# TensorE's loop over head pairs written out as straight code, with deeper buffers for weights and probabilities

## The chip, the cores and the metric

The kernel runs on one core of a Trainium2 chip. The metric is the device time of one execution in microseconds, as the median of several runs. One execution was also taken by the hardware profiler; its time and its span are given beside the median.

## What is computed

One decode step of an attention layer and an MLP in parallel, for 8 sequences with one token each. The model width D is 640, there are 32 heads of 128, 32 key and value heads, a cache of 4096 positions, and an MLP of 1728.

```
xn  = layernorm(x)
q   = (xn @ wq) as 8 x 32 heads x 128
s   = q . k_cache * 128**-0.5          # 8 x 32 x 4096
p   = softmax(s)
o   = p . v_cache                       # 8 x 32 x 128
y   = layernorm(xn)
h   = gelu(y @ w1 + b1)
out = x + o @ wo + h @ w2 + b2
```

All inputs and the output are bfloat16. Each key and value is used once, by one query, so nearly all of the 552 MB that are read are the two caches, 268 MB each.

## The kernel before

**Tiles.** A tile t (0 to 127) is one sequence and one pair of heads (HT = 2): 2 MB of K and 2 MB of V, on 128 partitions, 64 positions of 128 on each, in rows of 16 KB. The eight sequences of one head pair are eight tiles that follow each other; there are 16 head pairs (NG). Four tiles make a group (GT), whose softmax is done together; two groups make a head pair.

**Buffers.** KV_sb holds four K tiles and four V tiles (NK, NV). The V part is lent at first to the weights of the queries and of the MLP. wo_sb holds the rows of wo of one head pair. P_sb holds the probabilities of PR = 2 groups, S_sb the scores of three.

**Scores of a tile** (`scores`). VectorE makes the scores of 48 of the 64 positions: it multiplies the K tile with the query spread over the partitions (L534, into Y_sb), adds the halves (L538) and reduces (L541). TensorE makes those of the other 16: it transposes eight K blocks at a time (L502, into TR_ps), ScalarE copies them out (L505), and TensorE multiplies with the query (L512). The query for VectorE is broadcast by TensorE (`qbcast`, L471) from qb_sb; that for TensorE is read from qk_sb. Both are copies of the head pair's part of qT_sb, made on ScalarE by `qcopy` (L484).

**Softmax of a group** (`softmax`). VectorE takes the maximum (L549), TensorE transposes it (L551), VectorE reduces (L553), TensorE spreads it (L558), and ScalarE does the exponentials (L568). TensorE sums the parts (L579) and VectorE takes the reciprocal (L584, rinv_sb).

**Values of a tile** (`values`). Sixteen matmuls of 512 columns (L605), in four steps q of four, go into PV_ps; ScalarE copies it to E_sb (L613), and TensorE gathers the blocks into the output of the group (L621). The last tile of all loads its V in four pieces and uses 64 narrow matmuls of 128 columns (L602) with one gather (L619).

**Finish** (`finish`). VectorE scales the group's output (L629, oTn_sb). After each head pair but the last TensorE projects it through wo into an accumulator, transposed (L647). Before the last head pair is done, the accumulator with all other heads and the MLP is copied (L695), transposed back (L700), added to x and b2 (L707) and put into rows again (L713). The last head pair is projected straight onto those rows (L637), and the rows go out (L717, L719, L721).

**Order.** The order on each engine is fixed when the program is built. Each step has a position on one line of tile numbers: K tile t is loaded at t - 3.6 and scored at t; the values of tile i stand at `pvpos(i)`, which is 6.2 + i; V tile i + 4 is loaded at `pvpos(i)` + 0.95; wo of head pair hg is loaded at 8 hg + 7.2. `_Sched.solve` sorts the steps by position and works out the waits between engines. SP's queue issues all loads of K, V and the large weights in that order, each when its buffer is free: a K load waits for the scores of the tile four before, a V load for the values of the tile four before.

**TensorE's loop.** All engines run their steps as straight code, but TensorE doesn't. `emit_rolled` cuts TensorE's steps into windows of one head pair (eight positions, from 6.43), finds the longest run of windows that are alike, and writes that window once as the body of a loop. The values that its waits need rise by the same amount from window to window, so they are held in registers:

```
with e.Fori(0, j - i + 1):
    for o in body:
        for key, val in self.needs(o).items():
            e.reg_add(regs[key], regs[key], val - at[key])
            at[key] = val
            e.wait_ge(sems[key], regs[key])
        self.issue(o, e, sems)
```

The loop runs 15 times and takes in most of the scores and values; what stands ahead of it (the weights' work and the first tiles) and behind it (the last tiles) is straight code.

Of the kernel before, what the change touches and what calls it, by code (L numbers as in the profile page):

```python
# [6 lines left out]
BF = mybir.dt.bfloat16  # L7
# [4 lines left out]
P = 128  # L12
# [7 lines left out]
class _Sched:  # L20
# [79 lines left out]

    @staticmethod
    def needs(o):
        best = {}
        for d in o.waits:
            key = d.eng if d.sem is None else ("dma", d.sem)
            best[key] = max(best.get(key, 0), d.ticket)
        return best

    def emit(self, eng, e, sems, only=None):
        for o in self.ops if only is None else only:  # L110
            if o.eng != eng:
                continue
            for key, val in self.needs(o).items():
                e.wait_ge(sems[key], val)
            self.issue(o, e, sems)

    @staticmethod
    def issue(o, e, sems):
        last = o.fn(e)
        if o.sig:  # L120
            if o.sem is not None:
                last.then_inc(sems[("dma", o.sem)], 16)
            else:
                last.then_inc(sems[o.eng], 1)

    def emit_rolled(self, eng, e, sems, p0, step):

        ops = [o for o in self.ops if o.eng == eng]
        wins = {}
        for o in ops:
            if o.pos >= p0 and o.pos < 1e8:
                wins.setdefault(int((o.pos - p0) // step), []).append(o)

        def shape(w):
            return [(o.fn.__code__.co_firstlineno, o.sig, tuple(self.needs(o))) for o in w]  # L140

        def rise(a, b):
            return [tuple(nb[k] - na[k] for k in na) for na, nb in zip(map(self.needs, a), map(self.needs, b))]

        best = (0, 0)
        n = max(wins) + 1 if wins else 0
        for i in range(n):
            j = i
            while j + 1 < n and shape(wins[j + 1]) == shape(wins[i]) and (
                    j == i or rise(wins[j], wins[j + 1]) == rise(wins[i], wins[i + 1])):  # L150
                j += 1
            if j - i > best[1] - best[0]:
                best = (i, j)
        i, j = best
        if j - i < 2:
            self.emit(eng, e, sems)
            return
        body = wins[i]
        first, last = ops.index(body[0]), ops.index(wins[j][-1])
        self.emit(eng, e, sems, ops[:first])  # L160
        up = {}
        for o, r in zip(body, rise(body, wins[i + 1])):
            for key, d in zip(self.needs(o), r):
                assert up.setdefault(key, d) == d
        at = {}
        for o in body:
            at.update(self.needs(o))
        regs = {}
        for key in up:
            regs[key] = e.alloc_register("w%d" % len(regs))  # L170
            at[key] -= up[key]
            e.reg_mov(regs[key], at[key])
        with e.Fori(0, j - i + 1):
            for o in body:
                for key, val in self.needs(o).items():
                    e.reg_add(regs[key], regs[key], val - at[key])
                    at[key] = val
                    e.wait_ge(sems[key], regs[key])
                self.issue(o, e, sems)
        self.emit(eng, e, sems, ops[last + 1:])  # L180

# [19 lines left out]
def bass_parallel_sum__gqa_block_cached__mixer_channel_mlp__decode_kernel(  # L201
# [32 lines left out]
    NK, NV, NS = 4, 4, 4  # L234
    PR, SR = 2, 3
    assert DH == P and D % P == 0 and H % HT == 0 and B == 8 and NJ == 64 and H % 4 == 0
# [4 lines left out]
    with ExitStack() as es:  # L241
# [5 lines left out]
        KT_sb = sb("KT_sb", [P, NS, BK, P], BF)  # L247
        wo_sb = sb("wo_sb", [P, HT, D], BF)
        b1_sb = sb("b1_sb", [1, F], BF)
# [7 lines left out]
        qT_sb = sb("qT_sb", [P, H, B], BF)  # L257
        qb_sb = sb("qb_sb", [P, HT, B], BF)
        qk_sb = sb("qk_sb", [P, HT, B], BF)
        qbc_sb = sb("qbc_sb", [P, 2, GT, P], BF)  # L260
# [21 lines left out]
        rinv_sb = sb("rinv_sb", [P, 2, HT * GT], F32)  # L282
        oTn_sb = sb("oTn_sb", [P, HT, B], BF)
        resT_sb = sb("resT_sb", [P, DC * B], F32)
# [75 lines left out]
        def ld(pos, dst, src, W, sem, R=()):  # L360
            add("sp", pos, lambda e: e.dma_start(dst, src), R=R, W=W, sem=sem)
# [5 lines left out]
        if H > QP:  # L367
            ld(1.9, wqb_sb, A_wq[:, QP * P:H * P].rearrange("(c k) n -> k c n", k=P), ["wqB"], "wqb", ["ovfree"])

        def pvpos(i):  # L370
            return 6.2 + i

# [19 lines left out]
        for hg in range(NG):  # L392
            ld(hg * B + 7.2, wo_sb[:, :, :],
               A_wo[hg * HT * P:(hg + 1) * HT * P, :].rearrange("(a p) n -> p a n", p=P), ["wo"],
               "wo")

# [66 lines left out]
        def qbcast(g):  # L463
            hg, b0 = g // GPH, (g % GPH) * GT
            pos = g * GT - 1.3 if g else -55.0
            it = TRR.item()

            def pe(e):
                for i in range(GT):
                    for a in range(HT):  # L470
                        r = e.matmul(TRF[a * PG:(a + 1) * PG, it.box[0], i * P:(i + 1) * P],  # L471
                                     qb_sb[:, a, b0 + i:b0 + i + 1].to_broadcast([P, PG]),
                                     ident_bf[:, :], start=True, stop=True)
                return r
            add("pe", pos, pe, R=["qb", "ident"], W=[it], X=[it])
            add("act", pos + .01, lambda e: e.activation(  # L476
                qbc_sb[:, g % 2, :, :].rearrange("p g d -> p (g d)"), TRF[:, it.box[0], :], ACT.Copy),
                R=[it], W=[("qbc", g % 2)], X=[it])
        for g in range(NGRP):
            qbcast(g)  # L480


        def qcopy(hg, pos, dst, res):
            add("act", pos, lambda e: e.activation(dst[:, :, :], qT_sb[:, hg * HT:(hg + 1) * HT, :], ACT.Copy),  # L484
                R=[qt_res(hg * HT)], W=[res])
        for hg in range(NG):
            qcopy(hg, hg * B - 1.62 if hg else -56.0, qb_sb, "qb")
            qcopy(hg, hg * B - 0.62, qk_sb, "qk")


        def scores(t):
# [4 lines left out]
            def bank(n):  # L496
# [12 lines left out]
                def pe_qk(e):  # L509
                    for jj in range(BK):  # L510
                        c = (n * BK + jj) * HT
                        r = e.matmul(S_ps[:, c:c + HT], KT_sb[:, m % NS, jj, :],  # L512
                                     qk_sb[:, :, b], start=True, stop=True)
                    return r
                add("pe", t - 0.25 + 0.2 * n, pe_qk, R=[("KT", m % NS), "qk"], W=["S"], X=["S"])
            for n in range(MP):
# [109 lines left out]
        def finish(g):  # L626
            hg, b0 = g // GPH, (g % GPH) * GT
            np_ = pvpos(g * GT + GT - 1) + 0.85
            add("dve", np_, lambda e: e.tensor_tensor(  # L629
                oTn_sb[:, :, b0:b0 + GT], OT_ps.rearrange("p (a g) -> p a g", a=HT),  # L630
                rinv_sb[:, g % 2, :].rearrange("p (a g) -> p a g", a=HT), ALU.mult),
                R=["OT", ("rinv", g % 2)], W=["oTn"], X=["C2"])
            if g == NGRP - 1:
                def pe_last(e):
                    for a in range(HT):
                        for k in range(2):
                            r = e.matmul(TRF[0:B, k, 0:D // 2], oTn_sb[:, a, :],  # L637
                                         wo_sb[:, a, k * D // 2:(k + 1) * D // 2], start=False,
                                         stop=(a == HT - 1), skip_group_check=True)
                    return r  # L640
                add("pe", np_ + 0.3, pe_last, R=["wo", "oTn", "base_ps"], W=["fin"],
                    X=[("TR", 0), ("TR", 1)])
            elif (g + 1) % GPH == 0:
                def pe_o(e):
                    for a in range(HT):
                        for c in range(DC):
                            r = e.matmul(ACC_ps[:, c * B:(c + 1) * B], wo_sb[:, a, c * P:(c + 1) * P],  # L647
                                         oTn_sb[:, a, :], start=False,
                                         stop=(hg == NG - 2 and a == HT - 1 and c == DC - 1), skip_group_check=True)
                    return r  # L650
                add("pe", np_ + 0.32, pe_o, R=["wo", "oTn"], W=["ACC"], X=["ACC"])
        for t in range(T):
# [80 lines left out]
        @block.tensor  # L733
        def _(e):
            sch.emit_rolled("pe", e, sems, 6.43, B)

# [35 lines left out]
```

## Time and profile before

| | us |
|---|---|
| median of 3 runs | 1309.41 (1309.4 to 1309.8) |
| profiled execution, its own time | 1309.8 |
| its span, first to last instruction | 1308.0 |
| VectorE busy | 1111.0 (85%) |
| TensorE matmuls busy | 702.6 (54%) |
| ScalarE busy | 516.7 (39%) |
| read from HBM | 551.80 MB, 422 GB/s over the span |

A line of the page's DMA part has a queue, its kind, its packets, its megabytes, and the time that its packets took as a share of the span of all 16 DMA engines. A line of waits has the engine and line that waited, what it waited for, the total in microseconds, how often, and the longest. A piece of the chain has its start and its length in microseconds, the engine, the tile that it wrote, and the line.

### The profile page before, as it was taken

Reading aid. Unit: us, or ns where it says so; the run is one execution under the profiler, and the core shown is the slowest. Engines: PE = TensorE matmul, PEld = TensorE weight load, DVE = VectorE, ACT = ScalarE, POOL = GpSimd, SP = SyncE. Lnnn points to the kernel's source line nnn. Section 1 sums busy time; section 2 is a strip of 40 time slices with the busy share of each in tenths; the row PEclk is TensorE's granted clock in tenths of the full one; section 3 lists DMA queues with packets and bytes.
Section 4 is the critical chain, followed back from the end, with each engine's and each line's share of the span. In section 5 each row is a group of like instructions: output and inputs, shape, how many; then the busy total and the mean of one; then the engine's idle time right before and its main releaser. Section 6 shows DMA issues by size and latency. Waiting matters only on the chain.

```text
span 1308.0 us, 18464 instructions
## 1 busy us (share of the span) xinstructions
PE 702.6 (54%) x7741; PEld 400.7 (31%) x7741; DVE 1111.0 (85%) x554; ACT 516.7 (39%) x1264; POOL 0.2 (0%) x4
## 2 busy tenths in 40 slices
PE   2655555555455555545554555555455555546555
PEld 2533332233223223323332232332232323223222
DVE  7989889888898888898888898888988888988881
ACT  2443344433334333433434444344344334434332
POOL 0000000000000000000000000000000000000000
PEclk9995555555655555565555555555555555555555
DMA  9999999999999999999999999999999999999996
GB/s 373 424 427 424 428 427 428 428 427 428 427 428 426 426 430 426 428 426 429 428 427 426 426 431 427 426 430 427 427 427 427 430 427 425 427 430 427 426 429 272
DMA packets 45453, 552.14 MB, mean 422 GB/s; under 512 B 4505, under 2 KB 10993, under 8 KB 12786
## 3 DMA queue, kind: packets, MB, share of 16 engines
q1 hardware_dynamic: 45392, 551.81, 99.7%
q8 instruction: 10, 0.16, 0.1%
q14 instruction: 17, 0.14, 0.0%
q10 hardware_dynamic: 34, 0.02, 0.0%
HBM read 551.80 MB, written 0.01 MB: 422 GB/s over the span
## 4 chain that ended last, share of the span: by engine, by line
DMA 76%; DVE 14%; PE 9%; ACT 1%; issue 0%; SPq 0%
DMA KV_sb<-in_A_k_cache_dram 76%; DVE Y_sb L534 9%; PE TR_ps L502 5%; DVE S_sb L541 2%; PE C_ps L579 2%; PE PV_ps L605 2%; DVE Y_sb L538 1%; DMA KV_sb<-in_A_wq_dram 1%; DVE rinv_sb L584 0%; ACT P_sb L568 0%; ACT E_sb L613 0%; PE TR_ps L713 0%; PE PV_ps L602 0%; PE C_ps L621 0%; PE TR_ps L637 0%
## 5 line engine op out<-in xcount | busy, mean ns | idle before, releaser
L505 ACT ACTIVATE KT_sb<-TR_ps 128x1024 bf16<-128x1024 bf16 x256 | 261.3, 1023 | 645.7 <-PE TR_ps L502 645.3
L502 PE MATMUL TR_ps<-ident_bf,KV_sb 128*128 128x128 bf16 x2048 | 262.8, 310 | 425.0 <-DMA KV_sb<-in_A_k_cache_dram 425.0
L534 DVE TENSOR_TENSOR Y_sb<-KV_sb,qbc_sb 128x6144 bf16<-128x6144 bf16 x128 | 427.6, 3340 | 9.3 <-ACT qbc_sb L476 4.8
L541 DVE TENSOR_REDUCE S_sb<-Y_sb 128x48 f32<-128x3072 bf16 x128 | 429.2, 3353 | 4.4
L502 PEld LDWEIGHTS TR_ps<-ident_bf,KV_sb 128*128 128x128 bf16 x2048 | 196.9, 140 | 559.2 <-DMA KV_sb<-in_A_k_cache_dram 505.4
L605 PE MATMUL PV_ps<-KV_sb,P_sb 128*8 128x512 bf16 x2032 | 278.4, 582 | 39.2 <-DMA KV_sb<-in_A_v_cache_dram 39.0
L538 DVE TENSOR_TENSOR Y_sb<-Y_sb 128x3072 bf16<-128x3072 bf16 x128 | 224.1, 1750 | 2.3
L512 PE MATMUL S_ps<-qk_sb,KT_sb 128*128 128x2 bf16 x2048 | 90.4, 167 | 75.9 <-ACT KT_sb L505 75.9
L512 PEld LDWEIGHTS S_ps<-qk_sb,KT_sb 128*128 128x128 bf16 x2048 | 71.7, 104 | 129.9 <-ACT KT_sb L505 85.8
L584 DVE RECIPROCAL rinv_sb<-C_ps 128x8 f32<-128x8 f32 x32 | 6.6, 207 | 117.2 <-PE C_ps L579 117.2
L568 ACT ACTIVATE P_sb<-S_sb,NB_sb 64x64 bf16<-64x64 f32 x256 | 88.5, 346 | 4.2
L613 ACT ACTIVATE E_sb<-PV_ps 128x512 bf16<-128x512 f32 x128 | 75.6, 591 | 26.6 <-PE PV_ps L605 24.3
L605 PEld LDWEIGHTS PV_ps<-KV_sb,P_sb 128*8 128x8 bf16 x2032 | 39.6, 83 | 91.9 <-issue 45.2
L522 ACT ACTIVATE S_sb<-S_ps 64x16 f32<-64x16 f32 x256 | 45.4, 178 | 6.2 <-PE S_ps L512 4.7
L568 ACT ACTIVATION_READ_ACCUMULATOR P_sb<-S_sb,NB_sb 64x1 f32 x256 | 47.3, 185 | 0.0
L629 DVE TENSOR_TENSOR oTn_sb<-C_ps,rinv_sb 128x8 bf16<-128x8 f32 x32 | 5.3, 166 | 46.0 <-PE C_ps L621 36.7
L621 PE MATMUL C_ps<-sel_bf,E_sb 128*128 128x2 bf16 x508 | 33.1, 170 | 13.0 <-ACT E_sb L613 6.1
L562 ACT ACTIVATE NB_sb<-CH_ps 128x4 f32<-128x4 f32 x32 | 5.5, 173 | 73.8 <-PE CH_ps L558 73.8
L621 PEld LDWEIGHTS C_ps<-sel_bf,E_sb 128*128 128x128 bf16 x508 | 23.2, 105 | 28.1 <-ACT E_sb L613 28.1
L579 PEld LDWEIGHTS C_ps<-rs_sb,mask_f 128*128 128x128 f32 x128 | 31.2, 334 | 0.9 <-issue 0.9
L579 PE MATMUL C_ps<-rs_sb,mask_f 128*128 128x4 f32 x128 | 30.8, 346 | 0.0
L558 PE MATMUL CH_ps<-identneg,M_sb 4*64 4x4 f32 x128 | 11.3, 242 | 21.6 <-DVE M_sb L553 21.6
(81 smaller groups left out, 173.9 us busy)
## 6 DMA issues: line engine op xcount, KB each, us to landing
KV_sb<-in_A_k_cache_dram SPq DMA_DIRECT2D x128, 2048.0 KB, 34.1
KV_sb<-in_A_v_cache_dram SPq DMA_DIRECT2D x127, 2048.0 KB, 31.1
wo_sb<-in_A_wo_dram SPq DMA_DIRECT2D x16, 320.0 KB, 30.9
KV_sb<-in_A_wq_dram SPq DMA_DIRECT2D x1, 4480.0 KB, 17.2
KV_sb<-in_B_w_dram SPq DMA_DIRECT2D x1, 2160.0 KB, 19.3
KV_sb<-in_B_w_dram SPq DMA_DIRECT2D x1, 2080.0 KB, 24.4
KV_sb<-in_A_v_cache_dram SPq DMA_DIRECT2D x4, 512.0 KB, 10.9
KV_sb<-in_A_wq_dram SPq DMA_DIRECT2D x1, 640.0 KB, 9.6
```

Source lines behind the costliest of these rows:

```text
L502: r = e.transpose(TR_ps[:, it.box[0], jj * P:(jj + 1) * P], kv[:, n * BK + jj, :], ident_bf[:, :])
L505: add("act", t - 0.55 + 0.2 * n, lambda e: e.activation(KT_sb[:, m % NS, :, :].rearrange("p a b -> p (a b)"), TR_ps[:, it.box[0], :], ACT. ...
L512: r = e.matmul(S_ps[:, c:c + HT], KT_sb[:, m % NS, jj, :], qk_sb[:, :, b], start=True, stop=True)
L522: r = e.activation(S_sb[s, g % SR, i, 0:JP], S_ps[s, 0:JP * HT].rearrange("p (j a) -> p j a", a=HT)[:, :, a], ACT.Copy)
L534: return e.tensor_tensor(y, kv[:, j0:j1, :], qbc_sb[:, g % 2, i, :][:, None, :].to_broadcast([P, nj, P]), ALU.mult)
L538: lambda e, y=y, y2=y2: e.tensor_tensor(y2, y[:, :, 0:P // 2], y[:, :, P // 2:P], ALU.add),
L541: lambda e, y2=y2, j0=j0, j1=j1: e.tensor_reduce(S_sb[:, g % SR, i, j0:j1], y2, AX.X, ALU.add),
L568: r = e.activation(P_sb[s, g % PR, i, :, a, :], S_sb[s, g % SR, i, :].rearrange("p (m c) -> p m c", c=4), ACT.Exp, bias=NB_sb[s, g % 2, i: ...
L579: r = e.matmul(RS_ps[:, a * GT:(a + 1) * GT], mask_f[:, a, :], rs_sb[:, g % PR, :], start=True, stop=True)
L605: r = e.matmul(PV_ps[32 * ct:32 * ct + HT * 4, t % 2, :], P_sb[:, g % PR, i, m, :, :].rearrange("p a c -> p (a c)"), vv[:, 4 * m:4 * m + 4 ...
L613: add("act", p0 + 0.5, lambda e: e.activation(E_sb[:, t % 2, 0:ne], PV_ps[:, t % 2, 0:ne], ACT.Copy), R=[("PV", t % 2)], W=[("E", t % 2)], ...
L621: r = e.matmul(o, E_sb[:, t % 2, c * P:(c + 1) * P], sel_bf[:, c:HT * 4:4], start=(c == 0), stop=(c == 3))
```

## The change

`emit_rolled` is gone: TensorE's steps are written out one after the other like those of the other engines, and the waits have constant values again. With that, four other things are changed.

- The copies of the queries, qb_sb and qk_sb, are gone, with `qcopy`; TensorE reads qT_sb itself. Each head pair had two such copies on ScalarE, so that the loop's body could read one fixed place.
- wo_sb and oTn_sb have two halves that the head pairs use in turn, and wo's loads two semaphores.
- P_sb holds six groups instead of two (PR).
- The values' positions are stretched: `pvpos(i)` is 6.2 + 1.04 i, so that the values of the last tile stand at 138.3 instead of 133.2. The V loads, the projections and the final steps that hang on `pvpos` move with it; the scores and the K loads stay at their positions.

The projection of the last head pair onto rows and the narrow last tile are the same in both kernels.

```diff
-    def emit_rolled(self, eng, e, sems, p0, step):
...
-    PR, SR = 2, 3
+    PR, SR = 6, 3
...
-        wo_sb = sb("wo_sb", [P, HT, D], BF)
+        wo_sb = sb("wo_sb", [P, 2, HT, D], BF)
...
-        qb_sb = sb("qb_sb", [P, HT, B], BF)
-        qk_sb = sb("qk_sb", [P, HT, B], BF)
...
-        oTn_sb = sb("oTn_sb", [P, HT, B], BF)
+        oTn_sb = sb("oTn_sb", [P, 2, HT, B], BF)
...
+        CV = 1.04
+
         def pvpos(i):
-            return 6.2 + i
+            return 6.2 + CV * i
...
-            ld(hg * B + 7.2, wo_sb[:, :, :],
-               A_wo[hg * HT * P:(hg + 1) * HT * P, :].rearrange("(a p) n -> p a n", p=P), ["wo"],
-               "wo")
+            ld(hg * B + 7.2, wo_sb[:, hg % 2, :, :],
+               A_wo[hg * HT * P:(hg + 1) * HT * P, :].rearrange("(a p) n -> p a n", p=P), [("wo", hg % 2)],
+               "wo%d" % (hg % 2))
...
-                                     qb_sb[:, a, b0 + i:b0 + i + 1].to_broadcast([P, PG]),
+                                     qT_sb[:, hg * HT + a, b0 + i:b0 + i + 1].to_broadcast([P, PG]),
...
-        def qcopy(hg, pos, dst, res):
-            add("act", pos, lambda e: e.activation(dst[:, :, :], qT_sb[:, hg * HT:(hg + 1) * HT, :], ACT.Copy),
-                R=[qt_res(hg * HT)], W=[res])
-        for hg in range(NG):
-            qcopy(hg, hg * B - 1.62 if hg else -56.0, qb_sb, "qb")
-            qcopy(hg, hg * B - 0.62, qk_sb, "qk")
...
-                                     qk_sb[:, :, b], start=True, stop=True)
+                                     qT_sb[:, hg * HT:(hg + 1) * HT, b], start=True, stop=True)
...
-                add("pe", np_ + 0.32, pe_o, R=["wo", "oTn"], W=["ACC"], X=["ACC"])
+                add("pe", np_ + 0.3, pe_o, R=[("wo", hg % 2), ("oTn", hg % 2)], W=["ACC"], X=["ACC"])
...
-            sch.emit_rolled("pe", e, sems, 6.43, B)
+            sch.emit("pe", e, sems)
```

More of the change, by code (lines that the diff above doesn't have):

```diff
@@ L99, in solve, with emit @@
         return sorted(dcount)
[L101 to L110, printed above, removed]
+    def emit(self, eng, e, sems):
+        for o in self.ops:
             if o.eng != eng:
                 continue
-            for key, val in self.needs(o).items():
-                e.wait_ge(sems[key], val)
-            self.issue(o, e, sems)
@@ L117, in issue @@
[L117 to L124, printed above, removed]
-    def emit_rolled(self, eng, e, sems, p0, step):
[L133 to L180, printed above, removed]
@@ L183 @@
+            best = {}
+            for d in o.waits:
+                key = d.eng if d.sem is None else ("dma", d.sem)
+                best[key] = max(best.get(key, 0), d.ticket)
+            for key, val in best.items():
+                e.wait_ge(sems[key], val)
+            last = o.fn(e)
+            if o.sig:
+                if o.sem is not None:
+                    last.then_inc(sems[("dma", o.sem)], 16)
+                else:
+                    last.then_inc(sems[eng], 1)
 class _Ring:
@@ L471, in pe @@
                         r = e.matmul(TRF[a * PG:(a + 1) * PG, it.box[0], i * P:(i + 1) * P],
-                                     qb_sb[:, a, b0 + i:b0 + i + 1].to_broadcast([P, PG]),
+                                     qT_sb[:, hg * HT + a, b0 + i:b0 + i + 1].to_broadcast([P, PG]),
                                      ident_bf[:, :], start=True, stop=True)
                 return r
-            add("pe", pos, pe, R=["qb", "ident"], W=[it], X=[it])
+            add("pe", pos, pe, R=[qt_res(hg * HT), "ident"], W=[it], X=[it])
             add("act", pos + .01, lambda e: e.activation(
@@ L512, in pe_qk @@
                         r = e.matmul(S_ps[:, c:c + HT], KT_sb[:, m % NS, jj, :],
-                                     qk_sb[:, :, b], start=True, stop=True)
+                                     qT_sb[:, hg * HT:(hg + 1) * HT, b], start=True, stop=True)
                     return r
-                add("pe", t - 0.25 + 0.2 * n, pe_qk, R=[("KT", m % NS), "qk"], W=["S"], X=["S"])
+                add("pe", t - 0.25 + 0.2 * n, pe_qk, R=[("KT", m % NS), qt_res(hg * HT)], W=["S"], X=["S"])
             for n in range(MP):
@@ L629, in finish @@
             add("dve", np_, lambda e: e.tensor_tensor(
-                oTn_sb[:, :, b0:b0 + GT], OT_ps.rearrange("p (a g) -> p a g", a=HT),
+                oTn_sb[:, hg % 2, :, b0:b0 + GT], OT_ps.rearrange("p (a g) -> p a g", a=HT),
                 rinv_sb[:, g % 2, :].rearrange("p (a g) -> p a g", a=HT), ALU.mult),
-                R=["OT", ("rinv", g % 2)], W=["oTn"], X=["C2"])
+                R=["OT", ("rinv", g % 2)], W=[("oTn", hg % 2)], X=["C2"])
             if g == NGRP - 1:
@@ L636, in pe_last @@
                         for k in range(2):
-                            r = e.matmul(TRF[0:B, k, 0:D // 2], oTn_sb[:, a, :],
-                                         wo_sb[:, a, k * D // 2:(k + 1) * D // 2], start=False,
+                            r = e.matmul(TRF[0:B, k, 0:D // 2], oTn_sb[:, hg % 2, a, :],
+                                         wo_sb[:, hg % 2, a, k * D // 2:(k + 1) * D // 2], start=False,
                                          stop=(a == HT - 1), skip_group_check=True)
                     return r
-                add("pe", np_ + 0.3, pe_last, R=["wo", "oTn", "base_ps"], W=["fin"],
+                add("pe", np_ + 0.3, pe_last, R=[("wo", hg % 2), ("oTn", hg % 2), "base_ps"], W=["fin"],
                     X=[("TR", 0), ("TR", 1)])
@@ L646, in pe_o @@
                         for c in range(DC):
-                            r = e.matmul(ACC_ps[:, c * B:(c + 1) * B], wo_sb[:, a, c * P:(c + 1) * P],
-                                         oTn_sb[:, a, :], start=False,
+                            r = e.matmul(ACC_ps[:, c * B:(c + 1) * B], wo_sb[:, hg % 2, a, c * P:(c + 1) * P],
+                                         oTn_sb[:, hg % 2, a, :], start=False,
                                          stop=(hg == NG - 2 and a == HT - 1 and c == DC - 1), skip_group_check=True)
                     return r
-                add("pe", np_ + 0.32, pe_o, R=["wo", "oTn"], W=["ACC"], X=["ACC"])
+                add("pe", np_ + 0.3, pe_o, R=[("wo", hg % 2), ("oTn", hg % 2)], W=["ACC"], X=["ACC"])
         for t in range(T):
```

## The prediction

> **What bounds the kernel now.** I read the page first, then the DMA view in two stretches, the waits, the end of the chain, and last the records below these views: one landing record per transfer for each of the 16 DMA engines.
>
> The page:
>
> ```profile
> span 1308.0 us, 18464 instructions
> PE 702.6 (54%) x7741; PEld 400.7 (31%) x7741; DVE 1111.0 (85%) x554; ACT 516.7 (39%) x1264; POOL 0.2 (0%) x4
> DMA  9999999999999999999999999999999999999996
> q1 hardware_dynamic: 45392, 551.81, 99.7%
> q8 instruction: 10, 0.16, 0.1%
> q14 instruction: 17, 0.14, 0.0%
> ```
>
> No engine is full, but q1, which carries K, V and the weights, takes 99.7% of sixteen engines' span. Two small queues carry instructions. Where those are fetched shows in the DMA view of 0 to 160 us, then of 160 to 1270 us:
>
> ```profile
> q1 hardware_dynamic: 7848, 66.23, 99.5%
> q8 instruction: 8, 0.13, 0.3%
> ```
>
> ```profile
> DMA packets 36089, 474.59 MB, mean 428 GB/s; under 512 B 3812, under 2 KB 7396, under 8 KB 7396
> ...
> q1 hardware_dynamic: 36074, 474.46, 100.7%
> q14 instruction: 15, 0.12, 0.0%
> ```
>
> Queue 8 fetches eight 16 KB pages while TensorE runs its straight code (its first 2029 records, so 254 a page), none while it is in the loop (152 to 1267 us), and two more after it (1274.6 and 1296.8 us). So queue 8 is TensorE's. Queue 14's 8 KB pages are those of the others: ACT's come every 130 us or so, one per 128 of its records.
>
> What a page costs is in the landing records. A K or V tile puts eight 16 KB rows on each DMA engine, at 612 ns a packet 4.90 us a tile. The engines do not finish together, and the lag never shrinks. From first to last landing of one tile it is 1.1 us at 41 us, 2.1 at 101, 2.6 at 309, 3.3 at 458, 4.0 at 592, 5.3 at 864, 6.6 at 1101, 7.25 at 1235: one step of 0.66 us behind each of ACT's pages, always on the same engine. TensorE's pages make larger steps, each on another engine: among the sixteen lags 0.57 turns to 2.11 at the page of 98 us, 0.51 to 2.07 (119 us), 0.20 to 1.71 (142 us), 1.21 to 2.76 (1275 us), a mean of 1.54 us. The nine pages before the end hit nine different engines, none of them ACT's. A tile counts only when its last share is in, so the kernel runs at the pace of the one slowest engine, ACT's.
>
> Who waits:
>
> ```profile
> PEld TR_ps L502 <- DMA KV_sb<-in_A_k_cache_dram: 505.4, 121, 6.8
> PE TR_ps L502 <- DMA KV_sb<-in_A_k_cache_dram: 425.0, 120, 6.7
> DVE rinv_sb L584 <- PE C_ps L579: 117.2, 31, 5.0
> DVE oTn_sb L629 <- PE C_ps L621: 36.7, 30, 4.7
> ```
>
> TensorE waits for K tiles 425 us; VectorE waits for TensorE, which itself stands before a K tile. The end of the chain:
>
> ```profile
> 1301.46 0.27 PE C_ps L621 x4
> 1301.73 1.91 PE PV_ps L602 x64
> ...
> 1304.44 1.24 PE TR_ps L637 x4
> 1305.68 0.02 issue
> 1305.70 0.48 DVE out_sb L717
> ```
>
> The last V piece lands on the slowest engine at 1302.75 us, so 5.25 us of the span come after the stream.
>
> **The change part by part.** The profiled execution took 1309.8 us (span 1308.0 and 1.8 around it), the median is 1309.41; I add differences to the median.
>
> *Loop to straight code.* It takes away 780 register operations (32 ns each in the records, 25 us) and 15 jumps back (0.215 us each, 3.2 us) on TensorE's sequencer. Both lie under its 425 us of waiting for K: worth nothing. If that cover were gone they would be worth up to 28 us. It adds code: 7741 weight loads and 7741 matmuls are now each fetched once, with 45 separate waits (in the order of instructions as built) 15,530 records, at 254 to 256 a page some 60 or 61 pages against 9 before the stream's end; about 51 more. By the records they go round the engines (nine pages on nine engines), so 51/16 = 3.2 an engine, times 1.54 us = 4.9 us on average. What decides is ACT's engine: if the turn is sixteen long, its place is one of 10 to 16, then 26 to 32, 42 to 48 and 58 to 64. The fourth would mostly come too late, so three pages: 3 x 1.54 = +4.6 us; four would be +6.2. This engine has not a moment of idle time (4.90 us a tile, 79.2 us for 16 tiles and one wo transfer throughout), so nothing hides it. Bounds: from below the bytes alone, 51 x 16 KB = 0.84 MB at 428 GB/s, +2.0 us; from above seven pages' worth, if the turn is only the nine engines seen.
>
> [...]
>
> *q copies gone* (L484): 32 instructions of 216 ns on ACT, 7 us, under ACT's 61% idle; in the head 0.22 us before the first broadcast, while the first K tiles are queued anyway: nothing. ACT's code gets shorter by a quarter of a page; its step count stays.
>
> *P_sb six deep:* the memset grows from 0.48 us to some 1.45 us (three times the columns). VectorE stands idle 4.83 us right behind it: nothing.
>
> *wo_sb and oTn_sb double:* the 16 transfers of 0.77 us stay, a little earlier in SP's order; a transfer that starts earlier delays the K or V tile behind it by just what it delayed the other before. [...]
>
> *CV = 1.04:* the PV work falls behind the scores from 6.2 to 11 tiles. The K tiles come every 4.90 + 4.90/1.04 + 0.10 = 9.70 us instead of 9.90, and 12 V tiles instead of 7 follow the last K tile. The bytes are the same. VectorE needs 8.68 us a tile (1111/128), so it still waits. At the end only the four V buffers are in flight, three queued behind one in use: 14.7 us of work for the slowest engine against about 3 us from landing to release, so it doesn't run dry. Softmax of the last group, 11 us behind its last K tile, moves far ahead of the end; before, TensorE came late to the last tile (its q3 matmuls, a quarter of 1.91 us, could have ended at about 1303.3 and ended at 1303.64). Gain 0.3 us. The tail otherwise stays 5.25 us; the narrow last tile and the row-wise projection stand in both kernels.
>
> Sum: 1309.4 + 4.6 - 0.3 = 1313.7 us.
>
> **Rivals.** *Four pages on ACT's engine, or a turn over nine engines.* The second-slowest engine is 5.4 us behind the first and is one of the nine; with 51/9 = 5.7 pages more it would be 5.4 + 8.7 = 14.1 behind, 6.9 over ACT's 7.2: 1316.0. Four pages give 1315.2. For: nothing shows ACT's engine being hit; against: nine different engines without a repeat look like a longer turn.
>
> *Not slower: the stream's rate is set by memory, not by one engine.* Then what a page takes from one engine the others or the next tiles give back, and only the bytes count: 1309.4 + 2.0 - 0.3 = 1311.1, within the bound below. It decides if the first and last landings of the last tiles still lie no more than 7.3 us apart. For: the steady 428 GB/s. Against: lags kept for 1100 us without a shrink.
>
> *Faster: TensorE's order or sequencer was on the path.* At most the 28 us above, 1281. Against: the 425 us of DMA waits and 100.7% on q1.
>
> *Much slower: the shifted order starves the stream.* VectorE's work with its waits for TensorE is 8.68 + (117.2 + 36.7)/128 = 9.88 us a tile; if those waits stay when K comes every 9.70, the K phase keeps its old pace and the five extra V tiles behind it come on top: 5 x 4.90 = +24.5 us, 1333.6. It decides if DMA slices under 9 appear. Against: those waits are mostly TensorE standing before a K tile, and shrink when VectorE is late.
>
> **How the numbers follow.** The sixteen-turn with three or four pages 64%, a shorter turn 12%, bytes alone 13%, starved stream 8%, faster 3%. About 0.2% (2.6 us) is what a measurement of this kernel can tell from no change: slower 0.83, same 0.14, faster 0.03. The range holds bytes alone and the short turn with a little over: 1310.8 to 1317.2.
>
> **What would show it.** Right: q8 with about 60 pages, one each 20 us or so through the whole span; q1 at 99 to 100% and slices at 9 to the last; the last V tile's landings further apart than, or as far as, 7.3 us with the first of them some 4 us later; a tail of 5 us; no register work. A line saying that PE waits for "issue" for longer, or DMA slices at 8, would show TensorE short of instructions or the order at fault. A time under 1311 would make the step from pages to engine time wrong.

## The result, and the profile after

The changed kernel takes 1314.75 us (median, 1314.53 to 1315.31) against 1309.47 us for the kernel before on the same chip: ratio 1.0040, 95% interval 1.0023 to 1.0058. That is 5.3 us slower. The forecast was 1313.7, range 1310.8 to 1317.2.

The page of the kernel after:

```profile
span 1313.0 us, 17724 instructions
PE 695.8 (53%) x7741; PEld 407.7 (31%) x7741; DVE 1110.3 (85%) x554; ACT 512.9 (39%) x1232; POOL 0.2 (0%) x4
DMA  9999999999999999999999999999999999999997
q1 hardware_dynamic: 45392, 551.81, 99.4%
q8 instruction: 60, 0.98, 0.3%
q14 instruction: 18, 0.15, 0.0%
```

The engines do nearly the same work as before (ScalarE has the 32 copies of the queries less), and q1 moves the same bytes in the same number of packets. What differs is q8, TensorE's code: 60 pages in place of 10. The DMA view of the kernel after, 160 to 1270 us, where the kernel before had no q8 line at all:

```profile
DMA packets 36189, 472.55 MB, mean 426 GB/s; under 512 B 3800, under 2 KB 7640, under 8 KB 7640
...
q1 hardware_dynamic: 36123, 471.60, 100.2%
q8 instruction: 50, 0.82, 0.3%
q14 instruction: 16, 0.13, 0.0%
```

50 pages are 0.82 MB, under 0.2% of what moves in that stretch, and 0.3% of the engines' time by the packets' own durations. The waits of the kernel after (engine, line, what it waited for, total us, times, longest):

```profile
PEld TR_ps L430 <- DMA KV_sb<-in_A_k_cache_dram: 408.4, 117, 7.2
PE TR_ps L430 <- DMA KV_sb<-in_A_k_cache_dram: 351.5, 117, 7.1
PE PV_ps L533 <- DMA KV_sb<-in_A_v_cache_dram: 130.5, 68, 9.7
DVE rinv_sb L512 <- PE C_ps L507: 77.5, 28, 5.6
DVE oTn_sb L557 <- PE C_ps L549: 70.2, 23, 13.2
```

L430 is the old L502, L533 the old L605, L440 the old L512, L507 the old L579. TensorE's matmuls waited 425.0 us for K tiles before (the line in the prediction) and this long for V tiles:

```profile
PE PV_ps L605 <- DMA KV_sb<-in_A_v_cache_dram: 39.0, 60, 9.5
```

So TensorE waits for tiles at least as long as before, 482 us against 464; part of it has moved from the K to the V tiles, since the values now stand elsewhere in its order. It is not short of instructions either. The waits for "issue", in which nothing that the profile shows holds an engine back, first after, then before:

```profile
PEld S_ps L440 <- issue: 48.3, 121, 0.9
PEld TR_ps L430 <- issue: 39.9, 76, 0.8
PEld PV_ps L533 <- issue: 38.0, 175, 0.4
```

```profile
PEld TR_ps L502 <- issue: 53.8, 124, 0.8
PEld PV_ps L605 <- issue: 45.2, 220, 1.1
PEld S_ps L512 <- issue: 44.0, 120, 0.4
```

Together they are 126 us after and 143 before. VectorE's two waits for TensorE add up to 148 us, against 154 us: the shifted order starves nobody. The end of its chain (start, length, what):

```profile
1289.89 17.99 DMA KV_sb<-in_A_v_cache_dram
1307.89 0.04 issue
1307.93 0.70 PE PV_ps L530 x16
...
1309.43 1.24 PE TR_ps L565 x4
1310.67 0.02 issue
1310.70 0.48 DVE out_sb L645
```

The last V piece lands at 1307.89 us, before at 1302.75: 5.14 us later, in a span that is 5.0 us longer. From the last landing to the end it is 5.1 us, before 5.25.

The landing records say which engine was late. There are sixteen for each K or V transfer, one from each DMA engine; they hold times and no engine's name, so an engine is followed from tile to tile by how far it is behind the first one. Here are the sixteen of one V tile in each kernel, sorted, in us behind the first:

| | sixteen landings |
|---|---|
| before, first share at 1235.4 us | 0, 0.07, 0.14, 0.22, 0.69, 1.21, 1.37, 1.72, 1.73, 1.77, 1.98, 2.37, 2.42, 2.44, 4.45, 7.27 |
| after, first share at 1239.6 us | 0, 0.07, 0.23, 0.96, 1.00, 2.74, 4.65, 7.06, 10.99, 11.05, 11.13, 11.47, 11.58, 12.03, 12.59, 13.11 |

The engines of the kernel after fall into two sets: eight are 0 to 7.1 us behind the first, eight are 11.0 to 13.1 us behind. The 7.1 is ACT's engine, which still takes its steps of 0.66 us and none of TensorE's. The second eight share TensorE's pages in turn, each taking a step of 1.5 us at about every eighth page. So the slowest engine is now one of those eight, 13.1 us behind, where ACT's had been 7.25 behind. In the last tiles the engines draw together: the landings of the last V piece lie 7.1 us apart (1300.8 to 1307.9), before 6.4. The lag is therefore read ahead of them.

### The profile page after: what moved, and what is told of

The parts are those of the page before. It is cut to its first block, busy times and chain, and to the rows that moved or that the text cites. A ratio compares the mean times of both kernels' runs of the same rounds, so it can differ in the third digit from the quotient of the medians.

```text
span 1313.0 us, 17724 instructions
## 1 busy us (share of the span) xinstructions
PE 695.8 (53%) x7741; PEld 407.7 (31%) x7741; DVE 1110.3 (85%) x554; ACT 512.9 (39%) x1232; POOL 0.2 (0%) x4
## 4 chain that ended last, share of the span: by engine, by line
DMA 72%; DVE 18%; PE 8%; ACT 1%; issue 0%; SPq 0%
DMA KV_sb<-in_A_k_cache_dram 50%; DMA KV_sb<-in_A_v_cache_dram 21%; DVE Y_sb L462 10%; DVE S_sb L469 5%; PE TR_ps L430 3%; DVE Y_sb L466 3%; PE PV_ps L533 3%; PE C_ps L507 1%; DMA KV_sb<-in_A_wq_dram 1%; PE S_ps L440 0%; ACT P_sb L496 0%; PE TR_ps L407 0%; DVE rinv_sb L512 0%; ACT KT_sb L433 0%; DVE M_sb L477 0%
## 5 line engine op out<-in xcount | busy, mean ns | idle before, releaser
L433 ACT ACTIVATE KT_sb<-TR_ps 128x1024 bf16<-128x1024 bf16 x256 | 258.4, 1023 | 480.9 <-PE TR_ps L430 480.5
L430 PE MATMUL TR_ps<-ident_bf,KV_sb 128*128 128x128 bf16 x2048 | 256.2, 309 | 351.5 <-DMA KV_sb<-in_A_k_cache_dram 351.5
L533 PE MATMUL PV_ps<-KV_sb,P_sb 128*8 128x512 bf16 x2032 | 275.1, 589 | 130.9 <-DMA KV_sb<-in_A_v_cache_dram 130.5
L430 PEld LDWEIGHTS TR_ps<-ident_bf,KV_sb 128*128 128x128 bf16 x2048 | 198.3, 141 | 448.8 <-DMA KV_sb<-in_A_k_cache_dram 408.4
L440 PE MATMUL S_ps<-qT_sb,KT_sb 128*128 128x2 bf16 x2048 | 94.6, 168 | 53.9 <-ACT KT_sb L433 53.2
L440 PEld LDWEIGHTS S_ps<-qT_sb,KT_sb 128*128 128x128 bf16 x2048 | 75.8, 105 | 130.2 <-ACT KT_sb L433 81.7
L533 PEld LDWEIGHTS PV_ps<-KV_sb,P_sb 128*8 128x8 bf16 x2032 | 40.5, 85 | 181.3 <-DMA KV_sb<-in_A_v_cache_dram 140.4
L512 DVE RECIPROCAL rinv_sb<-C_ps 128x8 f32<-128x8 f32 x32 | 6.6, 207 | 77.5 <-PE C_ps L507 77.5
L549 PEld LDWEIGHTS C_ps<-sel_bf,E_sb 128*128 128x128 bf16 x508 | 28.1, 112 | 43.1 <-ACT E_sb L541 41.9
L507 PEld LDWEIGHTS C_ps<-rs_sb,mask_f 128*128 128x128 f32 x128 | 29.2, 316 | 9.1 <-issue 8.6
L507 PE MATMUL C_ps<-rs_sb,mask_f 128*128 128x4 f32 x128 | 31.0, 348 | 0.0
```

Of the source, the lines that this page charges most:

```text
L430: r = e.transpose(TR_ps[:, it.box[0], jj * P:(jj + 1) * P], kv[:, n * BK + jj, :], ident_bf[:, :])
L433: add("act", t - 0.55 + 0.2 * n, lambda e: e.activation(KT_sb[:, m % NS, :, :].rearrange("p a b -> p (a b)"), TR_ps[:, it.box[0], :], ACT. ...
L440: r = e.matmul(S_ps[:, c:c + HT], KT_sb[:, m % NS, jj, :], qT_sb[:, hg * HT:(hg + 1) * HT, b], start=True, stop=True)
L507: r = e.matmul(RS_ps[:, a * GT:(a + 1) * GT], mask_f[:, a, :], rs_sb[:, g % PR, :], start=True, stop=True)
L533: r = e.matmul(PV_ps[32 * ct:32 * ct + HT * 4, t % 2, :], P_sb[:, g % PR, i, m, :, :].rearrange("p a c -> p (a c)"), vv[:, 4 * m:4 * m + 4 ...
L549: r = e.matmul(o, E_sb[:, t % 2, c * P:(c + 1) * P], sel_bf[:, c:HT * 4:4], start=(c == 0), stop=(c == 3))
```

## The experiments

Theory A: a tile counts when the slowest of the sixteen DMA engines has brought its share, that engine has no idle time, and every page of code delays the engine that carries it: 1.54 us for one of TensorE's, dealt out over eight engines, and 0.66 us for one of ACT's, all on a ninth. Theory B: the pages cost their bytes. Theory C: the time comes from the stretched order or the deeper buffers. In text and table the lag is the largest between the first and the last landing of one K, V or wo transfer, over those whose first share landed between some 1100 and 1245 us, in the profiled execution.

**Straight code alone.**

```diff
-            sch.emit_rolled("pe", e, sems, 6.43, B)
+            sch.emit("pe", e, sems)
```

> The kernel before with one edit: TensorE's steps as straight code; query copies, single wo_sb, P_sb of two groups and unstretched positions stay. Theory A (the slowest DMA engine sets the time; each 16 KB page of TensorE's code costs the engine that carries it 1.54 us, and the pages go round eight engines that are not ACT's): some 60 pages, 7 to 8 on each of the eight, largest lag 13 us, 1309.5 + 5.3 to 5.9 = 1314.8 to 1315.4 us. Theory B (only the bytes count): 1309.5 + 2.0 = 1311.5. Theory C (the stretched positions or the deeper buffers cost the time): 1309.5.

Measured: 1315.13 us, ratio 1.0042 (1.0025 to 1.0059); 60 pages, lag 12.8 us. Writing out the loop makes the whole difference by itself.

**The kernel after without the stretch.**

```diff
-        CV = 1.04
+        CV = 1.0
```

> The kernel after with CV = 1.0 in place of 1.04. Theory A: the stretch is worth 0.1 to 0.3 us at the end, so 1314.8 to 1315.1 us, 60 pages, largest lag 13 us. Theory C: the time falls back towards 1309.5.

Measured: 1314.77 us, 60 pages, lag 12.6. The stretch is worth nothing that can be seen. With the run before, theory C falls.

**Half of the windows as straight code.**

```diff
         i, j = best
+        i = j - 6
```

> The kernel before with the loop over the last 7 of the 15 windows only; the first 8 are straight code. About 33 pages until the loop and 2 after it, 4 to 5 on each of eight engines. Theory A: these reach a lag of 0.4 to 0.7 + 5 x 1.54 = 8.1 to 8.4 us, against 7.25 for ACT's engine, so only the part above 7.25 is added: 1310.2 to 1311.0 us. Linear in the pages (25 of the 50 added, half of 5.3): 1312.1. Bytes alone: 1310.4, which this run does not tell from A; e1 and e4 do.

Measured: 1310.53 us, ratio 1.0010 (1.0000 to 1.0019). The page's q8 line, and the lag 8.4 us:

```profile
q8 instruction: 39, 0.64, 0.2%
```

29 of the 50 added pages (about 25 were expected) cost 1.1 us of the 5.3 to 5.7, by the interval 0 to 2.5; in proportion to the pages they would have cost about 3. That fits theory A: the first pages on an engine were free as long as ACT's engine was further behind, and the cost started where the eight passed 7.25 us (lag 8.4). It fits the bytes as well (1310.4 was expected for them); the next runs tell the two apart.

**More of TensorE's code, straight and in the loop.** The same edit in both kernels (here in the one after; before it is qk_sb):

```diff
                                      qT_sb[:, hg * HT:(hg + 1) * HT, b], start=True, stop=True)
+                    for _ in range(16):
+                        r = e.matmul(S_ps[:, 64:66], zeros_bf[:, :], zeros_bf[:, 0:2], start=True, stop=True)
                     return r
```

> The kernel after with 32 added matmuls of 2 columns per tile on zeros, into unused columns of S_ps: 8192 more records of TensorE, 32 more pages, 4 on each of the eight engines, and some 1 to 3 us of work per tile on an engine that waits for tiles. Theory A: + 4 x 1.54 = 6.2 us, 1320.9, largest lag 19 us. Theory B: 32 x 16 KB at 428 GB/s = +1.2, 1316.0. If TensorE's work counts at all, more than A.

> The kernel before, loop kept, with the same 32 added matmuls per tile as the run on the straight code. The loop's body grows to some 1470 records. Theory A: the work is the same as there, but the body is fetched once, so the pages rise by 2 to 4 in all and the time stays at 1309.3 to 1309.9 us. If TensorE's added work costs time, it does so here too and the time rises by as much as there.

Measured: on the straight code 1320.73 us (1320.58 to 1320.89), that is 6.0 over the kernel after, lag 20.1; in the loop 1309.32 us, ratio 0.9999 (0.9989 to 1.0008) to the kernel before. The pages' q8 lines and the added matmuls, straight code first:

```profile
q8 instruction: 92, 1.51, 0.5%
L443 PE MATMUL S_ps<-zeros_bf 128*128 128x2 bf16 x4096 | 143.5, 165 | 0.0
```

```profile
q8 instruction: 14, 0.23, 0.1%
L515 PE MATMUL S_ps<-zeros_bf 128*128 128x2 bf16 x4096 | 143.7, 165 | 0.0
```

The same 143 us of added matmuls cost nothing where the code is fetched once, and 6.0 us where 32 more pages are fetched: 4 pages for each of eight engines at 1.5 us. Bytes would be 1.2 us; theory B falls. (The profiled execution of the loop took 1311.34 us, the longest of the ten whose median is given. In it ACT's engine was already 2.1 us behind at 36 us, in the kernel before 0.6, and it was 9.2 behind near the end.)

**More of ACT's code, in both kernels.**

```diff
+        more_sb = sb("more_sb", [P, 128, 8], BF)
...
+            def act_more(e):
+                for n in range(8):
+                    r = e.activation(more_sb[:, t, n:n + 1], zeros_bf[:, 0:1], ACT.Copy)
+                return r
+            add("act", t + 0.7, act_more, R=["zeros"], W=["more"])
```

> The kernel before with 8 added one-column copies per tile on ScalarE (some 0.2 us each, 1.5 us of a tile's 9.9, ScalarE being 39% busy): 1024 more records, 8 more pages of 8 KB. Theory A: all on ACT's engine, which is the slowest: 8 x 0.66 = +5.3, 1314.8 us, largest lag 12.6. Theory B (bytes): +0.15, 1309.6. If ScalarE's work costs time: more than 0 in the run on the straight code as well.

> The kernel after with the same 8 added copies per tile on ScalarE. Theory A: ACT's engine goes from 7.1 to 12.4 us behind and is still not the slowest (13.1): 1314.5 to 1315.3 us, no change. If the cost of code were a sum over engines, or ScalarE's work counted: 1320.

Measured: on the kernel before 1315.32 us, ratio 1.0042 (1.0028 to 1.0056), lag 12.9; on the kernel after 1314.65 us (1314.49 to 1314.81), no change, lag 13.0. In the kernel before the page shows only this:

```profile
q8 instruction: 10, 0.16, 0.1%
q14 instruction: 25, 0.20, 0.0%
```

Eight pages of 8 KB, 66 KB in all, cost 5.7 us where their engine was the slowest, and nothing where it wasn't. Here the costs of code did not add up: the pages that cost 5.7 us alone added nothing to the 5.3 of TensorE's.

**A loop body twice as long.**

```diff
-            sch.emit_rolled("pe", e, sems, 6.43, B)
+            sch.emit_rolled("pe", e, sems, 6.43, 2 * B)
```

> The kernel before with a loop body of two head pairs (some 1910 records, 7.5 pages of 16 KB) in place of one (957 records, 3.7 pages), 7 times round. It asks how much code TensorE keeps. If it keeps this body: some 17 pages in all, 2 on an engine, lag below ACT's, 1309.3 to 1309.8 us. If not, it is fetched again each time round: some 60 pages and 1315 us.

Measured: 1317.91 us, ratio 1.0064 (1.0047 to 1.0081), worse than no loop; lag 16.0. The body was not kept, and both numbers that had been put for that case, some 60 pages and 1315 us, were too low. Its q8 line, and two of its waits:

```profile
q8 instruction: 78, 1.28, 0.4%
```

```profile
PEld TR_ps L502 <- issue: 98.7, 152, 5.7
PEld PV_ps L605 <- issue: 78.1, 221, 5.9
```

Each turn of 160 us fetches ten pages for a body of 7.6, three of them within 12 us at the jump back (237.2, 242.9, 249.0 us in the second turn), and TensorE stands still there: the six jumps back take 5.9 to 6.5 us each, in the kernel before 0.2, and the longest "issue" waits of these lines are 5.7 and 5.9 us, before 0.8 and 1.1. Even so the time follows the lag: against the straight code alone the lag is about 3 us more and the time 2.8. The bodies of one head pair (973 records) and of the run with added matmuls (1485) were not fetched again.

**ScalarE and VectorE in loops too.** If ACT's pages set the pace of the kernel before, it has the same reserve in it. For the loop a window's addresses must repeat, so S_sb gets two groups and the query copies go to GpSimd, which gets a program for them (its lines are left out here):

```diff
-    PR, SR = 2, 3
+    PR, SR = 2, 2
...
-            add("act", pos, lambda e: e.activation(dst[:, :, :], qT_sb[:, hg * HT:(hg + 1) * HT, :], ACT.Copy),
+            add("pool", pos, lambda e: e.tensor_copy(dst[:, :, :], qT_sb[:, hg * HT:(hg + 1) * HT, :]),
...
-            sch.emit("dve", e, sems)
+            sch.emit_rolled("dve", e, sems, 6.43, B)
...
-            sch.emit("act", e, sems)
+            sch.emit_rolled("act", e, sems, 6.43, B)
```

> The kernel before with ScalarE's and VectorE's steps in the same kind of loop as TensorE's. For that the score buffer S_sb has two groups instead of three, so that a window's addresses repeat, and the query copies are made on GpSimd. Theory A: ACT's and VectorE's pages in the body of the run are gone, the largest lag falls from 7.25 to 2.5 to 3 us (SP's engine and the pages of the straight parts), 1309.5 - 4.5 = 1305.0 us. Theory B (bytes: 13 pages of 8 KB less, 0.25 us): 1309.2. If register waits slow VectorE or the smaller S_sb holds it up: over 1309.5.

Measured: 1305.36 us, ratio 0.9968 (0.9956 to 0.9980), faster than both kernels; lag 2.5. Of the DMA view, 160 to 1200 us, the queue lines that are left:

```profile
q1 hardware_dynamic: 33781, 444.76, 100.7%
q14 instruction: 2, 0.02, 0.0%
```

Two runs take it apart. The first keeps the two other edits and takes both new loops out:

```diff
-            sch.emit_rolled("dve", e, sems, 6.43, B)
+            sch.emit("dve", e, sems)
...
-            sch.emit_rolled("act", e, sems, 6.43, B)
+            sch.emit("act", e, sems)
```

> The run with three loops, but ScalarE's and VectorE's steps as straight code again; the query copies on GpSimd and S_sb of two groups stay. It asks whether those two edits had a part in the 4 us gained. Theory A: no, ACT's engine is 7 us behind again (its code is a quarter of a page shorter) and the time is 1309.0 to 1309.6 us. If the two edits made the gain: 1305.4.

Measured: 1309.48 us, ratio 0.9999 (0.9990 to 1.0008), lag 7.1: those edits do nothing. The second takes out VectorE's loop alone (the first two lines of the diff above):

> The same with ScalarE's steps in a loop and VectorE's as straight code. Theory A: the slowest engine is now the one that carries VectorE's pages, 4.5 to 5.4 us behind in the runs so far, against 2.5 with both in loops and 7.25 with none: 1309.4 - 1.9 to 2.7 = 1306.7 to 1307.5 us. If only the number of pages counts: 10 of the 13 pages that the two loops save, 1306.3.

Measured: 1307.52 us, ratio 0.9985 (0.9976 to 0.9994), lag 5.2. The engine with VectorE's pages, 5.4 us behind in the kernel before, was next in line, and here it was the slowest.

All profiled executions, in the order of the lag:

| kernel | pages q8 | largest lag, us | last V landing, us | its own time, us | median, us |
|---|---|---|---|---|---|
| three loops | 10 | 2.5 | 1298.6 | 1305.5 | 1305.4 |
| TensorE's and ACT's loops | 10 | 5.2 | 1300.0 | 1307.5 | 1307.5 |
| before, S_sb of two, copies on GpSimd | 10 | 7.1 | 1303.1 | 1310.0 | 1309.5 |
| before | 10 | 7.3 | 1302.8 | 1309.8 | 1309.5 |
| half loop | 39 | 8.4 | 1303.1 | 1310.2 | 1310.5 |
| before, more of TensorE's code in the loop | 14 | 9.2 | 1304.4 | 1311.3 | 1309.3 |
| after, unstretched | 60 | 12.6 | 1307.9 | 1314.8 | 1314.8 |
| before, straight code | 60 | 12.8 | 1308.4 | 1315.3 | 1315.1 |
| before, more of ACT's code | 10 | 12.9 | 1308.4 | 1315.3 | 1315.3 |
| after, more of ACT's code | 60 | 13.0 | 1307.6 | 1314.5 | 1314.7 |
| after | 60 | 13.1 | 1307.9 | 1314.8 | 1314.8 |
| loop of two head pairs | 78 | 16.0 | 1310.5 | 1317.8 | 1317.9 |
| after, more of TensorE's code | 92 | 20.1 | 1313.7 | 1320.7 | 1320.7 |

From the first row to the last the lag grows by 17.5 us and the time by 15.2. It is not one to one. One part of that is that the engine that is measured against, the first one, isn't quite the same in each: the first share of K tile 126 lands at 1250.0 us with three loops and at 1249.3 in the loop of two head pairs. The rest was not looked into. In the run with more of TensorE's code in the loop, lag and time of the profiled execution go together like the others; the median stands for other executions.

## Why the prediction was right, step by step

- **The bound.** One engine of sixteen set the pace: shown by the runs with ACT's code (66 KB cost 5.7 us in one kernel and nothing in the other) and by the runs with more loops (lag 2.5 and 5.2 us, 1305.4 and 1307.5 us).
- **Pages and their price.** About 60 pages were forecast and 60 came; 1.54 us was forecast for one, and the 32 added pages cost 6.0 us over eight engines, 1.5 each.
- **Where the pages go.** This step failed. I took the nine pages of the kernel before to lie on nine engines and the turn to be sixteen long, with ACT's engine in it, and gave it three pages, 4.6 us. In the kernel after the turn was eight long and ACT's engine was not in it (eight engines were 11.0 to 13.1 us behind, ACT's 7.1). I had steps in the landing records for some of the nine only; the first page, at 19 us, came before the tiles that I followed. The records of the kernel before show the other eight on eight different engines (steps of 1.4 to 1.8 us at 46, 57, 71, 81, 101, 121, 146 and 1275 us). The engine of the last of these was furthest behind of all, 1.1 us, at 31 us already; that fits a first page on the same engine, and so a turn of eight. Of the lags that I listed, those at 41 and 101 us are therefore not ACT's, which was then 0.6 and 1.3 us behind; from 309 us on they are. A turn of eight puts 7 to 8 pages on each engine, and what counts is how far that passes ACT's engine: 13.1 - 7.25 = 5.9 us, where 5.3 was measured. So the mechanism of the rival with the shorter turn happened. Its 6.9 us were too high, as it put VectorE's engine into the turn: the one that was 5.4 us behind takes steps of 0.96 to 1.03 us behind four of queue 14's pages (364, 643, 961 and 1241 us) and none of TensorE's. (The other half of that rival, four pages on ACT's engine, adds up to 1315.3, not 1315.2.)
- **That 4.6 is near 5.3 is in part chance.** Three pages on the slowest engine and seven on one that starts lower come out alike. The half loop, at 1.1 us, is what tells the two apart: with ACT's engine in a turn of sixteen, half the added pages would have cost about half.
- **The sign for "the rate is set by memory"** was badly chosen. I asked how far apart the last tiles land; the last V piece, at 7.1 us, would have spoken for that rival. The tiles ahead of it (13.1 us) speak against it, and the runs with ACT's code settle it: 66 KB are 0.15 us at the 427 GB/s of that run (160 to 1240 us), and they cost 5.7.
- **The stretch at the end.** 0.3 us of gain was forecast. From the last landing to the end of the span it is 5.1 instead of 5.25 us, and in the medians it does not show (1314.75 stretched, 1314.77 not).
- **What was put at nothing** (register work, jumps, query copies, memset, wo halves, and 65 more waits on SP, whose records are 17 ns long in both kernels): the straight code alone gives 1315.13, the whole change 1314.75, and their runs overlap (1314.41 to 1315.30 and 1314.53 to 1315.31). Together these parts cost nothing that can be seen; they were not tried one by one.
- **What the fetch costs, and whom.** A page delayed the DMA engine that carried it by 1.5 us, and TensorE itself hardly at all: its "issue" waits at the three lines shown are 0.9 us at most in the kernel after. The jumps back of the kernel before and of the run with added matmuls, in bodies of 3.8 and 5.8 pages, started no fetch; those of the loop of two head pairs, 7.6 pages, did, and TensorE stood still for it.

## What to carry to other kernels

In a kernel like this one, whose loads are never idle, look at the sixteen landings of one transfer, not at the mean rate: the slowest DMA engine set the time here, and the code that it carried besides the data counted (eight more pages of ACT's, 5.7 us). Code that repeats was worth a loop here, first on the engine whose pages put their DMA engine furthest behind (ScalarE, from 1309.5 to 1307.5 us), then on the next one (VectorE, to 1305.4); but the body had to be short enough to be kept, and the one that was too long cost more than none (1317.9 us against 1315.1). Adding up the costs of several small things on different DMA engines was wrong here: the largest counted, and the same eight pages of ACT's were free in the kernel after.

## What the runs showed of the hardware that was not expected

- A 16 KB page of TensorE's code delayed its DMA engine by 1.5 us, though a 16 KB row of K took 0.61 us there and the page's own record is 1.06 us long on average. An 8 KB page of ACT's code delayed it by 0.66 us, with a record of 0.31 us.
- TensorE's pages went round eight engines in the kernel after (steps of about 1.5 us); ACT's all went to one (steps of 0.66), VectorE's to another (0.94 to 1.03 in the two kernels), neither among the eight.
- TensorE kept a loop body of 1485 records and did not keep one of 1944; for that it fetched ten pages a turn where 7.6 would hold it. Where in between the limit lies was not tried.
- Why a page of TensorE's took over twice the engine time of a row of equal size (1.5 us against 0.61) stays open.
